# Attention tiles: four heads' scores in one chain with four banks, and values summed per query tile in one bank

## The chip, the cores and the metric

The kernel runs on one core of one Trainium2 chip. Its engines work side by side: TensorE multiplies matrices and transposes, VectorE and ScalarE do element work (ScalarE the exponentials), GpSimd helps, and the DMA queues move data. The engines take their own instructions in program order and wait for one another by semaphores. The metric is the time of the whole program in microseconds (us), measured on the device; the time before is the median of three runs.

## The reference, cut to what matters

Four batches of eight heads, 768 positions and 64 values per head go through attention, in which a query sees the 128 positions up to its own and, besides, the first four of its sequence. Its result is the input of a layer of eight experts of which each token uses one, and that of a last layer with a sigmoid gate.

```python
scores = scale * np.matmul(q, k.transpose(0, 1, 3, 2))
is_sink = pos[None, :] < int(n_sink)                 # n_sink = 4
rel = pos[:, None] - pos[None, :]
in_window = (rel >= 0) & (rel < int(window))         # window = 128
scores = np.where(is_sink | in_window, scores, -1000000000.0)
a = np.exp(scores - np.max(scores, axis=-1, keepdims=True))
a = a / (np.sum(a, axis=-1, keepdims=True) + 1e-09)
return np.matmul(a, v).astype(np.float32)
...
x = attention's result, 3072 tokens of 512
e_idx = np.argmax(x @ w_gate + bias, axis=1)         # top-1 of 8 experts, F = 1024
out[mask] = gate_w[mask, None] * (np.maximum(x[mask] @ w1[e], 0.0) @ w2[e])
h = out @ w_in; g = h * (1.0 / (1.0 + np.exp(-1.702 * h))); return g @ w_out
```

## The kernel before

**Tiles.** Attention takes the 3,072 queries in 24 tiles `t` of 128, six to a batch (NT = 6; i = t % NT is the tile's place in its batch). A tile's queries see their own 128 keys, the 128 keys of the tile before (none where i = 0) and the four sink keys, so a row of scores is 128 or, with i > 0, 260 wide. `c` counts the four pairs of heads, `g` the two halves of four heads, `a` the two heads of a pair.

**Steps of a tile.** `load` brings q, k and v two tiles ahead. `qtrans` and `ktrans` transpose q and k on TensorE, `qevac` (ScalarE) and `kevac` (VectorE) copy them from the accumulation banks to SBUF. `scores` multiplies two heads, one on rows 0 to 63 of the array and one on rows 64 to 127, each into a bank of its own. `mask` (VectorE, L202) adds the mask and finds the row's extreme, `expo` (ScalarE, L211) takes the exponential and its sum. `ptrans` transposes a pair's weights with four products (L224, L225; L227 where i = 0), `pevac` copies them into `pts`, on VectorE for odd pairs (L242) and on ScalarE for even ones (L244). `pv` multiplies them with the values, each head of a pair on 64 columns of the array, into `ops`. `sinksplit`, `sinktrans` (L258, tile `stp`) and `sinkevac` (L263) prepare the weights of the sinks. `oevac` (ScalarE, L291) copies `ops` to `oh`; `back` (tile `bt`, L298 for the sinks and L301) turns the result back to tokens and makes the expert logits, `norm` (VectorE, L319) divides by the sum and sends the tile to DRAM; `logits`, `then` and `pick` choose the token's expert.

**How values are summed before.** A half `g` has a bank of `ops` of its own, which holds two query tiles side by side. The values of key tile t-1 are multiplied once with the weights of query tiles t-1 and t together, a moving operand of 256 columns. So a query tile's sum is complete only when `pv` has run for two steps, and for a batch's last tile L284 adds products of 128 columns. Since the products accumulate into what stands there, ScalarE writes zeros into each half of a bank first (`zero`, L268). `pts` is one buffer of three places (NG = 3) that is never given back, and `where`, `pview` and `psrc` find a tile's place in it.

**Banks.** The accumulation memory has eight banks: three in a ring for scores (`s`, NS_BUFS), three in a ring with the tag "t" that all of `qp`, `kp`, `pt`, `stp` and `bt` share (NT_BUFS), and two for `ops`. A step that takes a bank of a ring waits until the copy that empties its former use is done.

**What sets the order.** Nothing is reordered by a compiler. Every step is an entry of the list `todo`, with a time in slots, four slots to a tile: the first slot `n` that it covers, plus an offset from the table `AT`. The list is sorted, and each engine gets its instructions in that order. `kinds` gives each kind its size, that is how many slots one call covers:

```python
for nm, (size, fn) in kinds.items():
    for n in range(0, 4 * T, size):
        t, c = divmod(n, 4)
        ...
        todo.append((n + AT[nm] - sooner, fn, (t,) if size == 4 else (t, c) if size == 1 else (t, c // 2)))
```

**The end of attention.** The first pair of experts starts while the last tiles finish: `OPEN` places its steps on the same line of slots (`x0` and `x1` transpose the first gathered tokens, L1130; `split*` split weights into two parts; `first0` and `first1` are the first products, L1166), and `MORE` places the steps that sort the first experts' tokens and later the search that spreads tokens over blocks. The product `o_pp` on TensorE gives the places of the first tokens (`perm`), with which GpSimd gathers them (`xg`). When the last tile's expert is chosen (`pk_oh`, L672), L824 counts all tokens and the routing proper begins. After this come the remaining pairs of experts and the last layer, nearly all of it on TensorE.

Of the kernel before, what the change touches and what calls it, by code (L numbers as in the profile page):

```python
# [6 lines left out]
F32 = mybir.dt.float32  # L7
# [21 lines left out]

AT = dict(sinkevac=13.229, oevac=13.14, qevac=-3.201, kevac=-0.864, scores=-0.497, mask0=0.153, mask1=0.329, expo0=0.53, ptrans=2.608, pevac=3.3,  # L30
          expo1=1.235, pv=6.555, qtrans=-4.329, ktrans=-1.83, back=14.129, sinktrans=12.315, norm=14.975, logits=18.7, then=19.826, pick=23.746,
          guard=7.159, invert=12.135, zero=5.2, sinksplit=8.053)
PVU = 2
LATE = 0


OPEN = dict(split1=2.989, x0=5.244, split0=4.299, x1=5.358, split2=5.494, split3=6.448, first0=6.769, first1=7.711, split4=14.718)
MORE = 85.058, 0.617, 92.724, 1.445


def attention(tc, cst, late, first, spare, q, k, v, wg, xd, then, pick, at_tile, more, opening):
# [8 lines left out]
    with ExitStack() as ctx:  # L50
# [32 lines left out]
        m0, m1, m2 = cst["m0"], cst["m1"], cst["m2"]  # L83
        NV, NG = 6, 3
        zs = per.tile([P, 1], F32, name="zs")
        nc.gpsimd.memset(zs, 0.0)


        pts = per.tile([P, NG, 4, 2, 2, P], F32, name="pts")
        ops = [ps_o.tile([P, 2, 2, P], F32, name=f"ops{i}") for i in range(2)]  # L90

# [89 lines left out]

        def scores(t, c):

            i = t % NT
            x = qt[t][0]
            for a in range(2):
                r = slice(64 * a, 64 * a + 64)
                ps = ps_s.tile([P, 512], F32, name=f"s{t}_{c}_{a}", tag="s")
                scs[(t, 2 * c + a)] = ps
                if i == 0:  # L190
                    ks, n = kts[r, c, 0, 0:P], P
                else:
                    ks, n = kts[r, c, i - 1 : i + 1].rearrange("p j k -> p (j k)")[:, 0 : KB + P], KB + P
                nc.tensor.matmul(ps[:, :n], x[r, c, :], ks, start=True, stop=True)  # L194
# [17 lines left out]

        def where(t, kk):

            return kk if t % NG else 1 - kk

        def ptrans(t, c):
            i = t % NT
            ps = ps_t.tile([P, 2, 2, P], F32, name=f"pt{t}_{c}", tag="t")
            k0, k1 = where(t, 0), where(t, 1)  # L220
            for a in range(2):
                h = 2 * c + a
                if i > 0:
                    nc.tensor.transpose(ps[:, k0, a, :], pn[t][:, h, 0:P], ident)  # L224
                    nc.tensor.transpose(ps[:, k1, a, :], pn[t][:, h, KB : KB + P], ident)  # L225
                else:
                    nc.tensor.transpose(ps[:, k1, a, :], pn[t][:, h, 0:P], ident)  # L227
            tps[("p", t, c)] = ps

        def pview(t, c, x):  # L230
            if t % NT == 0:
                return x[:, t % NG, c, :, t % 2, :]
            a, b = sorted(((t - 1) % NG, t % NG))
            return x[:, a : b + 1 : b - a, c, :, t % 2, :]

        def psrc(t, c):
            ps = tps[("p", t, c)]
            return ps[:, where(t, 1)] if t % NT == 0 else ps

        def pevac(t, c):  # L240
            if c % 2:
                nc.vector.tensor_copy(pview(t, c, pts), psrc(t, c))  # L242
            else:
                nc.scalar.activation(out=pview(t, c, pts), in_=psrc(t, c), func=AF.Copy)  # L244

# [24 lines left out]
        def pv(t, g=None):  # L270

            i = t % NT
            if i == 0:
                return
            kw = dict(start=False, stop=False, skip_group_check=True)
            for j in [t - 1] + ([t] if i == NT - 1 else []):
                for h in range(H) if g is None else range(4 * g, 4 * g + 4):

                    c, a = divmod(h, 2)
                    o = ops[c // 2][64 * a : 64 * a + 64, c % 2]  # L280
# [61 lines left out]
        def fill(n):  # L342
            for _ in range(n):
                nc.tensor.matmul(ops[1].rearrange("p c i t -> p (c i t)")[:, 0:256], cst["nothing"][:, 0:P], cst["nothing"], start=True, stop=True)

        fill(F1)

        def ok(t):
            return 0 <= t < T


        kinds = dict(sinkevac=(4, sinkevac), oevac=(2, oevac), qevac=(4, qevac), kevac=(4, kevac), scores=(1, scores), mask0=(1, lambda t, c: mask(t, 2 * c)),
                     mask1=(1, lambda t, c: mask(t, 2 * c + 1)), expo0=(1, lambda t, c: expo(t, 2 * c)), expo1=(1, lambda t, c: expo(t, 2 * c + 1)),
                     ptrans=(1, ptrans), pevac=(1, pevac), pv=(PVU, pv), qtrans=(4, qtrans), ktrans=(4, ktrans), back=(2, back), sinktrans=(4, sinktrans), norm=(2, norm), logits=(4, logits), then=(4, lambda t: then(t, lgs.pop(t))), pick=(4, pick), guard=(4, guard), invert=(4, invert), zero=(2, zero), sinksplit=(4, sinksplit))
# [3 lines left out]
        for g in range(2):  # L358
            todo.append((len(F2) + .001, zero, (0, g)))
        for nm, (size, fn) in kinds.items():  # L360
            for n in range(0, 4 * T, size):
                t, c = divmod(n, 4)
                if nm in ("qtrans", "qevac", "ktrans", "kevac", "zero") and t == 0 or nm.startswith("sink") and t % NT < 2:
# [46 lines left out]
        todo.append((last("scores", "mask0", "mask1"), close, (sctx, "scores")))  # L410
        todo.append((last("pv", "zero", "expo0", "expo1"), close, (tctx, "values")))
        for nm, time in OPEN.items():
# [27 lines left out]

NS_BUFS = 3
NT_BUFS = 3
# [1198 lines left out]
```

## Time and profile before

| what | value |
|---|---|
| median of 3 runs | 1136.49 us (1130.78 to 1139.29) |
| profiled execution | 1139.11 us, its span 1137.5 us |
| TensorE busy | 1082.0 us, 95% of the span |
| VectorE, ScalarE, GpSimd busy | 553.5, 418.1 and 242.8 us |
| granted TensorE clock | 0.975 of 2.4 GHz on average |
| attention | about the first 224 us of the span |

An engine's share over the whole span says little about one stage: VectorE's 49% is 72% within the attention and much less behind it. What a change is worth in a stage is read from that stage's rows: which engine has no idle time there, and for whom the others wait. In the rows below `PE` is TensorE, `DVE` VectorE, `ACT` ScalarE and `POOL` GpSimd. A form such as 64*128 64x260 means that 64 rows and 128 columns of the array are used and the moving operand has 260 columns; a product in full precision is done in several passes, so its count in the trace is twice that of the instructions.

### The profile page before, as it was taken

How to read it: one execution, taken by the hardware profiler on the slowest of the kernel's cores; microseconds unless marked ns; L12 is line 12 of the kernel's file. 1: busy time of each engine (PE TensorE's matmuls, PEld its weight loads, DVE VectorE, ACT ScalarE, POOL GpSimd, SP SyncE). 2: the span in 40 equal slices, each digit the busy share in tenths (PEclk: the TensorE clock that was granted, in tenths of full speed). 3: DMA queues.
4: the chain of work that ended last, by engine and by line, in shares of the span. 5: the costliest groups of instructions: out<-in, count | busy, mean ns of one | idle time of the engine just before them, and what ended most of it. 6: DMA issues, size and time to landing. Idle time of an engine off the chain costs nothing. (4 is left out here: it accounts for less than half of the span.)

```text
span 1137.5 us, 18802 instructions
## 1 busy us (share of the span) xinstructions
PE 1082.0 (95%) x6625; PEld 916.0 (81%) x6625; DVE 553.5 (49%) x1385; ACT 418.1 (37%) x1026; POOL 242.8 (21%) x397
## 2 busy tenths in 40 slices
PE   7999999888999999999869999999999999999996
PEld 4676766578998999999867888888888888888885
DVE  3776677785544484522102566656533334234242
ACT  4887887643222342222112323323323222223221
POOL 2523131452332233211100222222210011011011
PEclk8999999988988999999979999999999999999999
DMA  6667677642777865435666313112023023033010
GB/s 119 130 114 134 127 118 108 147 78 62 125 90 100 195 129 104 57 57 162 106 166 179 111 41 126 45 67 75 2 74 111 10 102 112 1 111 136 13 38 37
DMA packets 172115, 108.49 MB, mean 95 GB/s; under 512 B 118000, under 2 KB 149744, under 8 KB 171984
## 3 DMA queue, kind: packets, MB, share of 16 engines
q1 hardware_dynamic: 167184, 91.43, 38.3%
q0 software_dynamic: 4800, 15.49, 4.3%
q8 instruction: 60, 0.98, 0.4%
q14 instruction: 71, 0.58, 0.2%
HBM read 79.61 MB, written 27.29 MB: 94 GB/s over the span
## 5 line engine op out<-in xcount | busy, mean ns | idle before, releaser
L1166 PE MATMUL pu<-xh,wah 128*128 128x256 f32 (+1 forms) x576 | 187.3, 325 | 0.0
L1166 PE MATMUL pu<-xh,wal 128*128 128x256 f32 (+1 forms) x576 | 185.8, 323 | 0.4 <-DVEq L1275 0.4
L1166 PE MATMUL pu<-xl,wah 128*128 128x256 f32 (+1 forms) x576 | 185.7, 322 | 0.0
L1551 DVE TENSOR_TENSOR raw<-pu,raw 128x512 f32<-128x512 f32 x96 | 66.3, 691 | 244.8 <-ACT raw L1550 210.4
L1550 ACT ACTIVATE raw<-pu 128x512 f32<-128x512 f32 x96 | 57.4, 598 | 291.9 <-PE pu L1166 286.8
L1181 PE MATMUL pa<-h,wah 128*128 128x256 f32 x768 | 158.4, 288 | 5.1 <-issue 5.1
L1181 PEld LDWEIGHTS pa<-h,wah 128*128 128x128 f32 x768 | 130.3, 197 | 4.1 <-issue 4.1
L1166 PEld LDWEIGHTS pu<-xh,wal 128*128 128x128 f32 x576 | 112.2, 195 | 8.4 <-DVEq L1275 0.6
L1166 PEld LDWEIGHTS pu<-xh,wah 128*128 128x128 f32 x576 | 112.2, 195 | 8.3 <-issue 0.4
L1166 PEld LDWEIGHTS pu<-xl,wah 128*128 128x128 f32 x576 | 112.1, 195 | 7.5
L1181 PE MATMUL pa<-h,wal 128*128 128x256 f32 x384 | 110.6, 288 | 1.9 <-issue 1.9
L1189 ACT ACTIVATE h<-pu 128x256 fp32r<-128x256 f32 x96 | 36.9, 384 | 200.0 <-PE pu L1166 177.0
L1192 DVE SCALAR_TENSOR_TENSOR h<-pu,h 128x256 fp32r<-128x256 f32 x96 | 40.5, 422 | 125.2 <-ACT h L1189 64.5
L202 DVE CUSTOM_DVE_ANT_0 sc<-s,m 128x260 f32<-128x260 f32 (+1 forms) x192 | 73.1, 399 | 52.8 <-PE s L194 46.9
L211 ACT ACTIVATE pn<-sc,mx 128x260 f32<-128x260 f32 (+1 forms) x192 | 92.0, 483 | 5.2 <-DVE mx L202 4.7
L1118 ACT ACTIVATE h<-raw 128x512 fp32r<-128x512 f32 x96 | 60.7, 632 | 77.7 <-DVE raw L1551 77.7
L1181 PEld LDWEIGHTS pa<-h,wal 128*128 128x128 f32 x384 | 75.8, 197 | 3.4 <-issue 3.4
L1173 PE MATMUL pa<-wah,h 128*128 128x512 f32 x216 | 76.3, 389 | 0.0
L1173 PE MATMUL pa<-wbh,h 128*128 128x512 f32 x216 | 76.3, 389 | 0.0
L1166 PE MATMUL pu<-xh,wbh 128*128 128x512 f32 x192 | 74.8, 390 | 1.0 <-ACT y L1489 1.0
L1166 PE MATMUL pu<-xh,wbl 128*128 128x512 f32 x192 | 74.8, 390 | 0.0
L1166 PE MATMUL pu<-xl,wbh 128*128 128x512 f32 x192 | 74.8, 390 | 0.0
(327 smaller groups left out, 2067.8 us busy)
## 6 DMA issues: line engine op xcount, KB each, us to landing
raw<-in_moe_w_dram SPq DMA_DIRECT2D x64, 256.0 KB
cd<-yb SPq DMA_DIRECT2D x20, 512.0 KB
xd<-xe SPq DMA_DIRECT2D x24, 256.0 KB
raw<-yp SPq DMA_DIRECT2D x12, 512.0 KB
qn<-in_q_dram SPq DMA_DIRECT2D x22, 256.0 KB
kn<-in_k_dram SPq DMA_DIRECT2D x22, 256.0 KB
vn<-in_v_dram SPq DMA_DIRECT2D x22, 256.0 KB
yb<-y SPq DMA_DIRECT2D x10, 512.0 KB
```

The costliest lines, as they stand in the source:

```text
L202: nc.vector.tensor_tensor_reduce(out=sc[:, :n], in0=ps[:, :n], in1=m[:, :n], scale=1.0, scalar=3.0e38, op0=ALU.add, op1=ALU.min, accum_out=mx)
L211: nc.scalar.activation(out=pn[t][:, h, :n], in_=sc[:, :n], func=AF.Exp, scale=-1.0, bias=mx, accum_out=sums[t][:, h : h + 1])
L1118: A.activation(out=hi, in_=x, func=AF.Copy)
L1166: nc.tensor.matmul(ps[:, 0:n], w[a][:, s], cols(x, b, k), start=(k == 0 and i == 0), stop=(k == 3 and i == 2))
L1173: nc.tensor.matmul(acc, h[a][:, s], w[b][:, 512:], start=(f == 0 and j == 0), stop=(f == last and j == 2))
L1181: nc.tensor.matmul(acc[:, i % 2 * 256 : i % 2 * 256 + 256], wa[f][a][:, s], h[b], start=(f == 0 and i % 2 == 0 and j == 0), stop=(f == CH ...
L1189: A.activation(out=hi, in_=ps, func=AF.Relu)
L1192: V.scalar_tensor_tensor(out=lo, in0=ps, scalar=0.0, in1=hi.bitcast(F32), op0=ALU.max, op1=ALU.subtract)
L1550: A.activation(out=s, in_=ps, func=AF.Sigmoid, scale=1.702)
L1551: V.tensor_tensor(out=s, in0=ps, in1=s, op=ALU.mult)
```

## The change

`scores(t, g)` now makes the scores of four heads one behind the other, in four banks (NS_BUFS 3 to 4). `pv(t, g)` sums the values for its own query tile alone: for each head a product of 128 columns with the values of the tile before and one with those of its own, begun and ended in one bank `ops` that holds all eight heads of one query tile. The zeroing goes, `pts` becomes a tile of its own for each t (two buffers), and the eight banks are now four, three and one. The tables are new: `pv` moves from 6.555 to 7.004, and as a tile's sum is complete a tile earlier, `oevac` goes from 13.14 to 10.224, `back` from 14.129 to 10.991, `norm` from 14.975 to 11.395 and the steps behind them in the same way.

```diff
-AT = dict(sinkevac=13.229, oevac=13.14, qevac=-3.201, kevac=-0.864, scores=-0.497, mask0=0.153, mask1=0.329, expo0=0.53, ptrans=2.608, pevac=3.3,
+AT = dict(sinkevac=10.229, oevac=10.224, qevac=-2.123, kevac=-1.366, scores=-0.449, mask0=-0.2, mask1=0.21, expo0=0.692, ptrans=2.608, pevac=3.437,
...
-OPEN = dict(split1=2.989, x0=5.244, split0=4.299, x1=5.358, split2=5.494, split3=6.448, first0=6.769, first1=7.711, split4=14.718)
-MORE = 85.058, 0.617, 92.724, 1.445
+OPEN = dict(split1=4.183, x0=5.146, split0=3.966, x1=5.358, split2=5.428, split3=6.826, first0=6.763, first1=6.923, split4=14.582)
+MORE = 84.738, 0.617, 92.724, 1.62
...
-        ops = [ps_o.tile([P, 2, 2, P], F32, name=f"ops{i}") for i in range(2)]
+        ops = ps_o.tile([P, 4, P], F32, name="ops")
...
-        def scores(t, c):
+        def scores(t, g):
...
-            for a in range(2):
+            for c, a in ((2 * g, 0), (2 * g, 1), (2 * g + 1, 0), (2 * g + 1, 1)):
...
+            if c == 0:
+                pts[t] = p2.tile([P, 4, 2, 2, P], F32, name=f"pts{t}", tag="pts")
...
-        def zero(t, g):
-
-            nc.scalar.activation(out=ops[g][:, :, t % 2, :], in_=zs.unsqueeze(2).broadcast_to([P, 2, P]), func=AF.Copy)
...
-                    if j == t - 1:
-                        nc.tensor.matmul(o.rearrange("p i t -> p (i t)"), nat[j]["v"][:, h], pts[:, j % NG, c, a].rearrange("p i t -> p (i t)"), **kw)
-                    else:
-                        nc.tensor.matmul(o[:, t % 2, :], nat[j]["v"][:, h], pts[:, j % NG, c, a, t % 2, :], **kw)
+            for c in (2 * g, 2 * g + 1):
+                for kk in range(i == 0, 2):
+                    for a in range(2):
+                        nc.tensor.matmul(ops[64 * a : 64 * a + 64, c], nat[t - 1 + kk]["v"][:, 2 * c + a], pts[t][:, c, kk, a], start=(kk == 0 or i == 0), stop=(kk == 1), skip_group_check=True)
...
-            nc.scalar.activation(out=ohl[t][:, 2 * g : 2 * g + 2], in_=ops[g][:, :, t % 2, :], func=AF.Copy)
+            nc.scalar.activation(out=ohl[t][:, 2 * g : 2 * g + 2], in_=ops[:, 2 * g : 2 * g + 2], func=AF.Copy)
...
-NS_BUFS = 3
+NS_BUFS = 4
```

TensorE's order before, at the first half of tile 10 (`s10_1_0` is tile 10, pair 1, head 0 of it; `pt9_1` is tile 9, pair 1; `x4` counts like instructions, and the number behind a name is only its place in the program):

```order
L194 MATMUL s10_0_0_2439<-kts_1140,qt10_2327 128x260
L194 MATMUL s10_0_1_2441<-kts_1140,qt10_2327 128x260
L224 MATMUL pt9_1_2444<-ident_97,pn9_2353 128x128
L225 MATMUL pt9_1_2444<-ident_97,pn9_2353 128x128
L224 MATMUL pt9_1_2444<-ident_97,pn9_2353 128x128
L225 MATMUL pt9_1_2444<-ident_97,pn9_2353 128x128
L156 MATMUL qp11_2449<-ident_97,qn11_2330 128x128 x4
L301 MATMUL bt6_1_2467<-btw_1123,oh6_2368 128x144 x2
L194 MATMUL s10_1_0_2479<-kts_1140,qt10_2327 128x260
L194 MATMUL s10_1_1_2481<-kts_1140,qt10_2327 128x260
L282 MATMUL ops1_1130<-pts_1128,vn7_1787 64x256 x4
```

Each group of two heads stands by itself, with transposes and `bt6_1` between the two; the half's values come behind the second. The same place on TensorE with the change:

```order
L258 MATMUL ops_1126<-pts8_2367,vn7_1839 64x128 x2
L258 MATMUL ops_1126<-pts8_2367,vn8_1992 64x128 x2
L191 MATMUL s10_0_0_2502<-kts_1136,qt10_2387 128x260
L191 MATMUL s10_0_1_2504<-kts_1136,qt10_2387 128x260
L191 MATMUL s10_1_0_2506<-kts_1136,qt10_2387 128x260
L191 MATMUL s10_1_1_2508<-kts_1136,qt10_2387 128x260
L216 MATMUL pt9_1_2510<-ident_97,pn9_2415 128x128
L217 MATMUL pt9_1_2510<-ident_97,pn9_2415 128x128
...
L153 MATMUL qp11_2515<-ident_97,qn11_2398 128x128 x4
L216 MATMUL pt9_2_2542<-ident_97,pn9_2415 128x128
L217 MATMUL pt9_2_2542<-ident_97,pn9_2415 128x128
...
L275 MATMUL bt7_1_2560<-btw_1123,oh7_2469 128x144 x2
```

The two score groups, between which transposes stood, are now one, and it follows the half's value products; the step `back` of an earlier tile has moved from ahead of the second score group to behind the second pair's transposes, and it now takes the bank of the ring that `pt9_1` had three uses before.

TensorE's order before, at the end of attention, around the first expert products (`x0` makes `pu1` and `pu2`, `first0` and `first1` are the products of `pu0` and `pu1`, of which the first and the last ones stand here):

```order
L1130 MATMUL pu2_4357<-ident_97,xg1_82 128x128
L298 MATMUL bt22_0_4537<-svb3_3525,stt22_4517 128x288
L301 MATMUL bt22_0_4537<-btw_1123,oh22_4515 128x144 x2
L1166 MATMUL pu0_4355<-xh0_4344,wah0_4361 128x256
...
L1166 MATMUL pu1_4356<-xl0_4345,wah1_4363 128x256
L298 MATMUL bt22_1_4583<-svb3_3525,stt22_4517 128x288
L301 MATMUL bt22_1_4583<-btw_1123,oh22_4515 128x144 x2
L258 MATMUL stp23_4588<-identr_1124,st23_4474 96x128
L298 MATMUL bt23_0_4596<-svb3_3525,stt23_4594 128x288
L301 MATMUL bt23_0_4596<-btw_1123,oh23_4592 128x144 x2
L298 MATMUL bt23_1_4610<-svb3_3525,stt23_4594 128x288
L301 MATMUL bt23_1_4610<-btw_1123,oh23_4592 128x144 x2
```

A half's turn back to tokens (`bt22_0`) stands between `x0` and `first0`, and three more behind `first1`. The same place on TensorE with the change:

```order
L272 MATMUL bt22_0_4604<-svb3_3638,stt22_4601 128x288
L275 MATMUL bt22_0_4604<-btw_1123,oh22_4599 128x144 x2
...
L272 MATMUL bt22_1_4639<-svb3_3638,stt22_4601 128x288
L275 MATMUL bt22_1_4639<-btw_1123,oh22_4599 128x144 x2
...
L1102 MATMUL pu2_4504<-ident_97,xg1_82 128x128
L244 MATMUL stp23_4687<-identr_1124,st23_4631 96x128
L1138 MATMUL pu0_4502<-xh0_4491,wah0_4508 128x256
...
L1138 MATMUL pu1_4503<-xl0_4492,wah1_4510 128x256
L272 MATMUL bt23_0_4725<-svb3_3638,stt23_4691 128x288
L275 MATMUL bt23_0_4725<-btw_1123,oh23_4689 128x144 x2
L272 MATMUL bt23_1_4742<-svb3_3638,stt23_4691 128x288
L275 MATMUL bt23_1_4742<-btw_1123,oh23_4689 128x144 x2
```

Tile 22's turn back to tokens, half of which stood between `x0` and `first0` and half behind `first1`, has moved ahead of `x0`; behind `first1` only tile 23's is left. Ahead of `o_pp` now stand the sink transpose and the first half's `back` of tile 21 and one half of tile 22's values, which came behind it.

## Rows read from the trace of the kernel before

**Rows 1.** Windows, attention and after: busy us (instructions) by engine, clock, DMA

```profile
24.00:224.00 200.00, 198.94 (x1504) 135.43 (x1502) 144.08 (x598) 161.15 (x546) 66.01 (x208) 1.00 0.69 119
224.00:244.00 20.00, 11.47 (x80) 10.99 (x81) 12.75 (x27) 8.67 (x15) 10.21 (x13) 0.91 0.73 167
```

**Rows 2.** Waits of TensorE, 24 to 224 us: total, times, longest

```profile
PE stp L258 <- DVE pts L242: 0.6, 1, 0.6
```

**Rows 3.** Timeline of TensorE, one tile: start, us, operation, tiles, forms, count

```profile
94.48 0.27 PE L225 MATMUL pt<-ident,pn 128*128 128x128 f32 x1
94.68 0.71 PE L194 MATMUL s<-kts,qt 64*128 64x260 f32 x4
95.32 0.33 PE L224 MATMUL pt<-ident,pn 128*128 128x128 f32 x1
95.49 0.27 PE L225 MATMUL pt<-ident,pn 128*128 128x128 f32 x1
95.60 0.27 PE L224 MATMUL pt<-ident,pn 128*128 128x128 f32 x1
...
96.25 0.66 PE L301 MATMUL bt<-btw,oh 128*128 128x144 f32 x4
96.84 0.71 PE L194 MATMUL s<-kts,qt 64*128 64x260 f32 x4
97.48 1.08 PE L282 MATMUL ops<-pts,vn 128*64 128x256 f32 x8
98.49 0.33 PE L224 MATMUL pt<-ident,pn 128*128 128x128 f32 x1
```

**Rows 4.** Timeline of TensorE at a batch's last tile

```profile
67.33 1.08 PE L282 MATMUL ops<-pts,vn 128*64 128x256 f32 x8
68.25 0.61 PE L284 MATMUL ops<-pts,vn 128*64 128x128 f32 x8
68.79 0.44 PE L227 MATMUL pt<-ident,pn 128*128 128x128 f32 x2
```

**Rows 5.** Groups of instructions, 24 to 224 us: busy us, mean ns, idle before

```profile
L242 DVE COPY pts<-pt 128x512 f32<-128x512 f32 x40 | 27.6, 690 | 5.7 <-PE pt L225 4.7
...
L268 ACT ACTIVATE ops<-zs 128x256 f32<-128x256 f32 x46 | 17.8, 387 | 1.4
```

**Rows 6.** Timeline of VectorE: one score group, two stretches of the end

```profile
138.11 0.43 DVE L202 CUSTOM_DVE_ANT_0 sc<-s,m 128x260 f32<-128x260 f32 x1 [1.01 <-PE s L194]
...
138.60 0.69 DVE L242 COPY pts<-pt 128x512 f32<-128x512 f32 x1
...
216.10 0.64 DVE L242 COPY pts<-pt 128x512 f32<-128x512 f32 x1
...
237.82 2.38 DVE L675 CUSTOM_DVE_ANT_0 pk_d<-lg,bias 128x8 f32<-128x8 f32 x1 [0.30 <-POOL lg L330]
...
240.80 1.96 DVE L678 SCALAR_TENSOR_TENSOR pk_eq<-pk_d,pk_mx,c_rank 128x8 f32<-128x8 f32 x1
```

**Rows 7.** Timeline of TensorE: that score group, then the end

```profile
137.26 0.71 PE L194 MATMUL s<-kts,qt 64*128 64x260 f32 x4
...
216.80 0.27 PE L258 MATMUL stp<-identr,st 128*96 128x128 f32 x1 [0.58 <-DVE pts L242]
...
228.25 1.75 PE L1130 MATMUL pu<-ident,xg 128*128 128x128 f32 x7 [1.67 <-ACT xg L1139]
...
230.83 0.55 PE L1166 MATMUL pu<-xh,wah 128*128 128x256 f32 x1
...
233.98 0.29 PE L298 MATMUL bt<-svb,stt 96*128 96x288 f32 x1
...
236.03 0.37 PE L298 MATMUL bt<-svb,stt 96*128 96x288 f32 x1 [1.20 <-DVE xe L319]
...
237.26 0.38 PE L1166 MATMUL pu<-xh,wah 128*128 128x256 f32 x1
...
243.79 0.24 PE L824 MATMUL pt<-pk_oh,c_ones 128*128 128x192 bf16 x1 [3.41 <-DVE pk_oh L672]
```

More of the change, by code (lines that the diff above doesn't have):

```diff
@@ L83, in attention @@
         m0, m1, m2 = cst["m0"], cst["m1"], cst["m2"]
[L84 to L89, printed above, removed]
-        ops = [ps_o.tile([P, 2, 2, P], F32, name=f"ops{i}") for i in range(2)]
+        NV = 6
+        ops = ps_o.tile([P, 4, P], F32, name="ops")
+        pts = {}
         sctx = ctx.enter_context(ExitStack())
@@ L223, in ptrans @@
                 if i > 0:
-                    nc.tensor.transpose(ps[:, k0, a, :], pn[t][:, h, 0:P], ident)
-                    nc.tensor.transpose(ps[:, k1, a, :], pn[t][:, h, KB : KB + P], ident)
+                    nc.tensor.transpose(ps[:, 0, a, :], pn[t][:, h, 0:P], ident)
+                    nc.tensor.transpose(ps[:, 1, a, :], pn[t][:, h, KB : KB + P], ident)
                 else:
-                    nc.tensor.transpose(ps[:, k1, a, :], pn[t][:, h, 0:P], ident)
+                    nc.tensor.transpose(ps[:, 1, a, :], pn[t][:, h, 0:P], ident)
             tps[("p", t, c)] = ps
[L230 to L238, printed above, removed]
         def pevac(t, c):
+            if c == 0:
+                pts[t] = p2.tile([P, 4, 2, 2, P], F32, name=f"pts{t}", tag="pts")
+            k = slice(1, 2) if t % NT == 0 else slice(0, 2)
+            x, ps = pts[t][:, c, k], tps.pop(("p", t, c))[:, k]
             if c % 2:
-                nc.vector.tensor_copy(pview(t, c, pts), psrc(t, c))
+                nc.vector.tensor_copy(x, ps)
             else:
-                nc.scalar.activation(out=pview(t, c, pts), in_=psrc(t, c), func=AF.Copy)
+                nc.scalar.activation(out=x, in_=ps, func=AF.Copy)
         stt, sts = {}, {}
@@ L343, in fill @@
             for _ in range(n):
-                nc.tensor.matmul(ops[1].rearrange("p c i t -> p (c i t)")[:, 0:256], cst["nothing"][:, 0:P], cst["nothing"], start=True, stop=True)
+                nc.tensor.matmul(ops.rearrange("p c t -> p (c t)")[:, 0:256], cst["nothing"][:, 0:P], cst["nothing"], start=True, stop=True)
         fill(F1)
@@ L349, in ok @@
             return 0 <= t < T
-        kinds = dict(sinkevac=(4, sinkevac), oevac=(2, oevac), qevac=(4, qevac), kevac=(4, kevac), scores=(1, scores), mask0=(1, lambda t, c: mask(t, 2 * c)),
+        kinds = dict(sinkevac=(4, sinkevac), oevac=(2, oevac), qevac=(4, qevac), kevac=(4, kevac), scores=(2, scores), mask0=(1, lambda t, c: mask(t, 2 * c)),
                      mask1=(1, lambda t, c: mask(t, 2 * c + 1)), expo0=(1, lambda t, c: expo(t, 2 * c)), expo1=(1, lambda t, c: expo(t, 2 * c + 1)),
-                     ptrans=(1, ptrans), pevac=(1, pevac), pv=(PVU, pv), qtrans=(4, qtrans), ktrans=(4, ktrans), back=(2, back), sinktrans=(4, sinktrans), norm=(2, norm), logits=(4, logits), then=(4, lambda t: then(t, lgs.pop(t))), pick=(4, pick), guard=(4, guard), invert=(4, invert), zero=(2, zero), sinksplit=(4, sinksplit))
+                     ptrans=(1, ptrans), pevac=(1, pevac), pv=(2, pv), qtrans=(4, qtrans), ktrans=(4, ktrans), back=(2, back), sinktrans=(4, sinktrans), norm=(2, norm), logits=(4, logits), then=(4, lambda t: then(t, lgs.pop(t))), pick=(4, pick), guard=(4, guard), invert=(4, invert), sinksplit=(4, sinksplit))
         todo = []
@@ L357, in attention @@
             todo.append((n + AT["scores"] + .001, fill, (some,)))
-        for g in range(2):
-            todo.append((len(F2) + .001, zero, (0, g)))
         for nm, (size, fn) in kinds.items():
@@ L362, in attention @@
                 t, c = divmod(n, 4)
-                if nm in ("qtrans", "qevac", "ktrans", "kevac", "zero") and t == 0 or nm.startswith("sink") and t % NT < 2:
+                if nm in ("qtrans", "qevac", "ktrans", "kevac") and t == 0 or nm.startswith("sink") and t % NT < 2:
                     continue
@@ L410, in attention @@
         todo.append((last("scores", "mask0", "mask1"), close, (sctx, "scores")))
-        todo.append((last("pv", "zero", "expo0", "expo1"), close, (tctx, "values")))
+        todo.append((last("pv", "expo0", "expo1"), close, (tctx, "values")))
         for nm, time in OPEN.items():
```

17 lines of the change are left out of this document (3 added, 14 removed).

## Prediction

> **What bounds the kernel now.** I read first the windows of the attention [rows 1]: between 24 and 224 us TensorE is busy for 198.94 of 200 us, at the full clock (1.00, that is 2.4 GHz), while VectorE has 144.08 and ScalarE 161.15. Then the waits: in those 200 us TensorE waits for one thing once, 0.6 us [rows 2]. So in the attention the bound is TensorE's own stream. What is taken off its stream shortens the stage; what is taken off ScalarE or VectorE gives nothing as long as they keep up. Only behind it, from 224 to 244 us, does TensorE stand still: 11.47 of 20 us busy [rows 1]. There it waits for the gathered tokens, for VectorE and, 3.41 us long, for the last tile's choice [rows 7]. From then on it is again almost always at work, so that a shift of this point passes to the end. The sum is made against the profiled execution, 1139.11 us (span 1137.5), 2.6 above the median of 1136.49; I carry the difference over to the median.
>
> **Changes of shape on TensorE (a gain of 14.0 us).** Within tile 10 the same product costs more at its place than in a row [rows 3]. A transpose takes 0.11 us from start to start inside a group (95.49 to 95.60). By columns, 260 against 128, one pass of a score pair is 0.22, and the two passes of a group 0.44. But from the last transpose before the scores (94.48) to the second one behind them (95.49) it is 1.01 us, where 0.11 + 0.44 + 0.11 = 0.66 would do: a visit from transposes on 128 rows to scores on 64 rows and back costs 0.35. The longer visit, scores, then values on 64 columns, then transposes, costs 0.49 by the same reading: 96.25 to 98.49 is 2.24, of which `bt`, four times 0.12 at its 144 columns, takes 0.48, scores 0.44 and values 0.88 (four passes of two heads at 0.22), which leaves 0.44; with the slow first transpose (0.05 more) it is 0.49. A tile now makes two visits of each kind, 1.68 us in all. With the change scores and values still meet, in the other order, and the lonely score groups are gone: two visits of the long kind, 0.98. Saved: two times 0.35, 0.70 per tile, in the 20 tiles with 260-wide scores 14.0 us. The step from values straight to scores is in no row. Its cost lies between nothing (0.10 less per half: the entry of 0.20 at 94.48 to 94.68 less the usual 0.11) and a full visit of its own (0.20 more per half); I take the reverse order's, its nearest row. For the four tiles with 128-wide scores I count nothing: their groups have no row here, and 0.3 each is the most.
>
> **Values with 128 columns (nothing).** Each instruction of 256 columns becomes two of 128, each with its own weight load. At a batch's last tile both kinds stand next to each other [rows 4]: eight records of 256 columns take 0.92 to the next start, eight of 128 columns 0.54 including the way out. Both together take 1.46, and the wide ones alone took 1.01 [rows 3], so the narrow ones add 0.45, half of a wide group's 0.88 and a hair. The columns in all stay the same, and so does the time. The Trainium skill ("TensorE: Matmul & The Clock Gate", section "Back-to-back issue gap") speaks against the change: the spacing of load and multiply pairs is set by both, about 81 ns at 128 columns and 131 at 512, so that a narrow product is dearer per column. By an even line between these two figures, an estimate, 256 columns are 98 ns, and two narrow ones would cost 1.65 times a wide one. By that the value groups would grow from 0.88 to 1.45, 0.57 per half, 22.8 us in 20 tiles; that is the last rival below, against which the narrow group speaks [rows 4].
>
> **Zeroing (nothing).** 17.8 us of ScalarE go [rows 5], but TensorE does not wait for ScalarE. What this gives is room on ScalarE, 161 to about 143 us of a stage that itself gets shorter.
>
> **A new wait at the ring of three banks (a loss of 3.2 us).** In a half the order is now scores, four transposes, q (or k), four transposes, `back`. `back` needs the bank that the first four transposes filled, and thus VectorE's copy of it; before, a score group and the values lay between. From the chain's start: 0.64 for the first two heads with the way in and out [rows 3] and 0.44 for the others, so the transposes start at 1.08, the fourth at 1.08 + 0.17 + 0.22 = 1.47, and it ends 0.27 later [rows 3], at 1.74. VectorE has by then just made two masks: the first starts 0.85 behind a score group's start (137.26 to 138.11), lasts 0.43, and the next follows it [rows 6, 7], which ends near 1.65. Its copy lasts 0.69 [rows 5, 6] and TensorE goes on 0.06 after such a copy has ended (216.74 to 216.80) [rows 6, 7]: ready at 2.51. `back` could start at 1.08 + 0.49 + 0.44 + 0.44 = 2.45, since four transposes take 0.49 after scores and 0.44 in a row. The wait is 0.06 to 0.08 per half; I take 0.08, times 2 and 20. Behind `back` stand the values and the next score chain, for which masks and exponentials wait, so nothing hides it. Its ends are 0, if the copy is that much earlier, and 0.19, if the way into the scores costs 0.10 less, as above; but then the first term is larger by the same, and the two ends cancel.
>
> **The four score banks.** There is no spare bank: the next chain's last two heads use banks that this chain's last two masks must have left. On VectorE the copy ends at 2.46, the two masks behind it at about 3.3, and where a copy of keys, of the same size, comes before one of them, near 4.0; the next chain comes about 4.2 later and needs these banks half a microsecond after that. I count nothing, with that slack as the cover; its loss is a rival.
>
> **The end of attention (nothing, net).** Ahead of `o_pp` now stand a sink transpose (0.2), half a `back` (0.6 by 96.25 to 96.84, with its sink product 0.8) and half a tile of values (0.9): 1.9 us later, with everything that the gathered tokens start [rows 3, 7]. Against this, the `back` of tile 22 no longer stands between `x0`, which starts at 228.25, and `first0` at 230.83, about 0.8; and of the 3.28 us between the start of the first `back` behind `first1` (233.98) and the next expert product (237.26), of which 1.20 is a wait for VectorE, about 1.2 stay [rows 7]. TensorE's part is 2.9 us shorter. But L824 waits 3.41 us for VectorE's choice, whose steps are stretched to 2.38 and 1.96 us [rows 6], and how much this chain gives is in no row: from nothing to the whole 2.9, and with the stretching gone as much as 5. I take 1.9, which cancels the later `o_pp`, since the choice follows tile 23's `back`, which comes earlier.
>
> **The sum.** -14.0 + 3.2 + 1.9 - 1.9 = -10.8: 1128.3 for the profiled execution, 1125.7 on the median, 1.0% faster, at the edge of what a measurement of this kernel tells from no change (about 1%).
>
> **Rivals.** (1) More is gained: the ring's wait does not bind and the end gives its whole 5 us: -14.0 + 1.9 - 5 = -17.1, 1119. For it: the computed wait is a few hundredths. Against it: the 0.6 us in which TensorE did wait is for just this copy [rows 2]. (2) It is spent again: the step from values to scores costs a second full change, 0.20 per half (8.0 us), and `back` waits 0.19 (7.6): -14.0 + 8.0 + 7.6 + 1.9 - 1.9 = +1.6, 1138; with one of the two, 1130 to 1134. For it: each entry into a shape costs at its place, and nothing shows this one. (3) Slower: VectorE, which has 72% of the time [rows 1] of a stage that gets 5% shorter, falls behind within the half, and the chain waits for its last masks. It decides from a lag of 0.5 us, the slack above; one more copy of 0.69 or two masks ahead of it do it, and then each half stands about 0.5, 1.0 per tile, 24 us in 24 tiles: 1125.7 + 24 = 1150. Against it: the order on VectorE puts the masks nearly evenly. (4) Slower: each narrow product takes as long as the wide one, because its weight load bounds it; by 0.88 per half that is 35 us, 1161. Against it stands the narrow group [rows 4].
>
> **How the numbers follow.** The forecast has 0.45 (its own range 1119 to 1132, half of it on either side of 1125.1, where 1% begins), the larger gain 0.15, the spent gain 0.27, the VectorE lag 0.10, the dear narrow products 0.03. Faster by over 1% is the larger gain and half of the forecast, 0.38; slower 0.13; within 1% the rest, 0.49. The range goes from 1115, the first rival with the cheap step from values to scores (0.10 per half, 4 us), to 1139, the spent gain; it leaves the two slower cases out.
>
> **What would show it.** In the windows: attention ends about 9 us earlier with TensorE still over 97% busy. In TensorE's timeline of a tile: a score group of eight records of about 1.1 us, with no transposes between two groups, and value groups still near 1.0 (1.45 or more is rival 4). In TensorE's waits: a row of `bt` (or `stp`) for VectorE's `pts`, some 40 times, 3 us in all; 8 us would be rival 2. A row of TensorE `s` waiting for VectorE's `sc` or `mx` would be rival 3. At the end: `first0` closer behind `x0`, and L824's wait of 3.41. I am wrong if the chain's handshakes cost what the fewer changes of shape give, or if the step from values to scores is a full change.

## The result and the profile after

The changed kernel took 1115.11 us (median of 4 runs) beside 1135.45 for the kernel before on the same chip: a ratio of 0.983, 95% interval 0.980 to 0.986. That is 20 us, twice what was forecast (10.8), at the lower edge of the range (1115). The same kernel, measured twice more beside the kernel before, gave 1123.71 (0.991, 0.987 to 0.994) and 1122.82 (0.992, 0.989 to 0.995): 9 to 10 us. The three medians of the kernel before in these sets were 1135.45, 1134.02 and 1133.16, so the first set is the odd one on the changed kernel's side.

The windows that answer to [rows 1], from the changed kernel's profile:

```profile
24.00:224.00 200.00, 194.56 (x1835) 155.17 (x1833) 143.56 (x600) 150.46 (x500) 65.83 (x210) 0.99 0.84 128
224.00:244.00 20.00, 16.72 (x110) 16.05 (x110) 16.92 (x49) 9.05 (x17) 11.29 (x8) 0.82 0.43 84
```

TensorE has idle time by now, but the first window no longer lies within the attention: the last tile's scores start at 201.72 us where it was 206.59. TensorE's waits in it are still few; the first row, for the gathered tokens `xg`, belongs to the end of attention, and without it they come to 1.2 us (0.6 before [rows 2]):

```profile
PE pu L1102 <- ACT xg L1111: 3.7, 2, 3.4
PE pt L216 <- DVE pts L228: 0.6, 2, 0.3
PE o_pp L737 <- DVE raw L731: 0.4, 1, 0.4
PE bt L275 <- ACT oh L265: 0.2, 1, 0.2
```

Tile 10 on TensorE, which answers to [rows 3], and VectorE beside it, which answers to [rows 6]:

```profile
92.48 1.15 PE L191 MATMUL s<-kts,qt 64*128 64x260 f32 x8
93.56 0.33 PE L216 MATMUL pt<-ident,pn 128*128 128x128 f32 x1
...
94.71 0.27 PE L216 MATMUL pt<-ident,pn 128*128 128x128 f32 x1
94.82 0.27 PE L217 MATMUL pt<-ident,pn 128*128 128x128 f32 x1
95.09 0.73 PE L275 MATMUL bt<-btw,oh 128*128 128x144 f32 x4
95.75 1.09 PE L258 MATMUL ops<-pts,vn 128*64 128x128 f32 x16
96.78 1.15 PE L191 MATMUL s<-kts,qt 64*128 64x260 f32 x8
97.85 0.27 PE L244 MATMUL stp<-identr,st 128*96 128x128 f32 x1
```

```profile
93.33 0.43 DVE L199 CUSTOM_DVE_ANT_0 sc<-s,m 128x260 f32<-128x260 f32 x1 [0.95 <-PE s L191]
...
94.26 0.69 DVE L228 COPY pts<-pt 128x512 f32<-128x512 f32 x1
```

The four heads are one group of eight records, 1.08 us to the next start, and the sixteen narrow value records take 1.03, as the eight wide ones did (1.01). Between the last transpose (94.82) and `bt` (95.09) lie 0.27 us where two transposes lie 0.11 apart. VectorE's copy starts at 94.26, 1.78 behind the chain's start, where the prediction has it (its end at 2.46 less 0.69), but `bt` starts 0.83 behind the copy's start, not 0.75. No wait is listed for it: the transpose's modelled end is 95.09, so the row shows no idle time, and only the distance of the starts does. Over 38 such places between 42 and 200 us the distance is 0.21 us on average; in the variant E2 below, where nothing waits, it is 0.06 (0.11 where the next row is L275, 0.03 where `bt` begins with the sinks' product L272).

The end of attention, which answers to [rows 7]:

```profile
210.01 0.44 PE L737 MATMUL o_pp<-o_bt,raw 128*128 128x2 f16 x12
...
222.67 1.75 PE L1102 MATMUL pu<-ident,xg 128*128 128x128 f32 x7 [3.35 <-ACT xg L1111]
...
224.33 0.52 PE L1138 MATMUL pu<-xh,wah 128*128 128x256 f32 x1
...
228.91 0.30 PE L272 MATMUL bt<-svb,stt 96*128 96x288 f32 x1
...
230.33 0.37 PE L1138 MATMUL pu<-xh,wah 128*128 128x256 f32 x1
...
236.72 0.26 PE L796 MATMUL pt<-pk_oh,c_ones 128*128 128x192 bf16 x1 [3.28 <-DVE pk_oh L644]
```

Against [rows 7], `o_pp` comes 5.7 us earlier (215.67 before), `first0` starts 1.66 behind `x0`'s last row where it was 2.58, the first `back` behind `first1` 1.42 ahead of the next expert product where it was 3.28, and L796 (L824 before) 7.07 us earlier, with its wait for VectorE's choice hardly changed (3.28, 3.41 before).

So only 7 of the profile's 24 us were there when the routing starts. To see where the others came from I counted TensorE's product records from L824 (L796) on; there are 4,950 of them in each kernel, in the same order, so that the same number is the same work. Start of the routing and length of five stretches, in us, from each run's trace (the fillings are explained with the experiments):

```
run                          routing  0-500  500-930  930-2360  2360-2700  2700-4949
before                        243.8    66.4    68.4     171.0      65.2      512.7
changed                       236.7    66.3    55.4     171.0      61.0      512.8
E1  changed again             237.6    67.7    52.4     174.1      66.8      512.8
E11 changed, third time       237.6    67.1    53.4     172.6      66.0      512.8
E2  groups of two             242.7    66.4    57.4     171.0      64.7      512.8
E3  shared copy               242.1    66.4    53.4     172.4      66.9      512.8
E8  back behind the values    235.1    66.5    56.1     175.4      61.9      512.7
E5  before again              242.4    65.0    60.2     170.9      66.3      512.7
E6  before, new OPEN, MORE    243.8    68.0    59.4     172.8      66.2      512.8
E9  before, 128 fillings      244.0    65.9    60.5     171.1      65.7      512.7
E7  before, 59 fillings       244.9    67.2    55.5     172.9      66.2      512.7
E10 before, 59 fillings again 246.0    66.2    54.2     173.0      61.9      512.7
E4  changed, 69 fillings      235.7    66.1    58.1     171.9      73.2      513.0
E12 changed, 69, again        236.1    66.5    61.2     171.1      63.4      512.8
```

The stretch from 500 to 930 (the first pairs of experts behind the search) gave 13 us of the first profiles' 24, where I had counted on a shift that just passes through. What TensorE waits for there, first in the profile before and then in the changed one, 290 to 385 us:

```profile
PE pa L1181 <- issue: 6.6, 8, 2.1
PE pt L1130 <- ACT xs L1149: 2.5, 2, 1.6
```

```profile
PE pu L1138 <- issue: 1.6, 4, 0.4
```

The largest stop of the profile before looks like this in TensorE's timeline: products 1.4 us apart, with the weight load of each 0.70 ahead of it, and no releaser:

```profile
312.85 0.28 PE L1181 MATMUL pa<-h,wah 128*128 128x256 f32 x1 [2.15 <-issue]
314.25 0.37 PE L1181 MATMUL pa<-h,wal 128*128 128x256 f32 x1 [1.12 <-issue]
315.64 0.37 PE L1181 MATMUL pa<-h,wah 128*128 128x256 f32 x1 [1.03 <-issue]
```

### The profile page after: what moved, and what is told of

It reads as the page before. It is cut to its first block, busy times and chain, and to the rows that moved or that the text cites. A ratio compares the mean times of both kernels' runs of the same rounds, so it can differ in the third digit from the quotient of the medians.

```text
span 1113.2 us, 19356 instructions
## 1 busy us (share of the span) xinstructions
PE 1069.4 (96%) x6945; PEld 928.7 (83%) x6945; DVE 551.3 (50%) x1385; ACT 405.8 (36%) x978; POOL 243.1 (22%) x396
## 4 chain that ended last, share of the span: by engine, by line
PE 46%; issue 4%; DMA 1%; POOL 0%; POOLq 0%; ACT 0%; DVE 0%; SPq 0%; ACTq 0%
PE pu L1138 22%; PE pa L1145 16%; PE pu L1145 5%; DMA raw<-in_moe_w_dram 1%; PE pu L1450 1%; PE pa L1459 1%; POOL out_dram L1547 0%; POOLq L1609 0%; PE pt L1102 0%; DVE raw L1523 0%; ACT raw L1522 0%; ACT ca L1452 0%; POOLq L1547 0%; SPq L1067 0%; ACTq L1522 0%
## 5 line engine op out<-in xcount | busy, mean ns | idle before, releaser
L1522 ACT ACTIVATE raw<-pu 128x512 f32<-128x512 f32 x96 | 57.4, 598 | 291.8 <-PE pu L1138 290.3
```

The lines of the kernel that those rows point to most:

```text
L1522: A.activation(out=s, in_=ps, func=AF.Sigmoid, scale=1.702)
```

## Experiments

All are compared with the kernel before on the same chip; medians in us, ratio with its 95% interval. A batch is the time from the first scores of one batch's first tile to the next batch's, here from the third to the fourth: 51.51 before, 49.76 with the change, within 0.01 in every profile of either.

**E1, the changed kernel again** (no edit).

> The changed kernel unaltered, as the base of this set. The changed kernel's first profile ended 24 us earlier than the profile of before; only 7.1 us of it were there when the routing starts (the product with the last tile's choice, 243.79 to 236.72), and 12.6 us more came between 303 and 377 us of before, where TensorE stood with no releaser named. If that later gain belongs to the change, this run is again near 1115 us with only short stops of TensorE between 290 and 370 us; if it is chance from execution to execution, the stops come back here or the time moves by 5 us or more.

Measured: 1123.71, ratio 0.991. The stops stayed away, stretch 500 to 930 took 52.4 us, the routing started at 237.6, yet the time was 8.6 us above the first set. In the traces the difference lies in 930 to 2700 (8.9 us more). In that stretch TensorE stood 18.8 us where it stood 11.9 in the first profile (the longest wait is L1450's for expert weights, `in_moe_w_dram`: 10.5 us against 8.0), and it was busy for 222.1 us at a granted clock of 0.96 against 220.1 at 0.98. So the stretch from 500 to 930 is the change's in some way, and another part of the first 20 us was not.

**E2, scores in groups of two.**

```diff
-        def scores(t, g):
+        def scores(t, pair):
...
-            for c, a in ((2 * g, 0), (2 * g, 1), (2 * g + 1, 0), (2 * g + 1, 1)):
+            for c, a in ((pair, 0), (pair, 1)):
...
-        kinds = dict(... scores=(2, scores), ...
+        kinds = dict(... scores=(1, scores), ...
```

> The changed kernel with the scores again in groups of two heads, the second group at the slot where a second pair's step stands; values, banks and tables as changed. It puts one lonely visit to the scores' shape back into each half tile. Theory A (changes of shape are the gain): 0.35 us per half more on TensorE, about 0.7 per tile, less the wait of the turn back to tokens for the copy (0.16 per half in the changed kernel's profile), which the visit covers: a batch of six tiles goes from 49.8 to about 52 us, the attention ends 7 to 9 us later, the time is near 1123. Theory B (the gain is from elsewhere, such as the freed zeroing or the narrow values): the batch stays within 0.5 us of 49.8.

Measured: 1127.91, ratio 0.995 (0.992 to 0.997); batch 51.61, routing at 242.7. The timeline of its tile:

```profile
95.32 0.33 PE L216 MATMUL pt<-ident,pn 128*128 128x128 f32 x1
...
96.34 0.71 PE L191 MATMUL s<-kts,qt 64*128 64x260 f32 x4
96.98 0.33 PE L216 MATMUL pt<-ident,pn 128*128 128x128 f32 x1
...
97.37 0.27 PE L217 MATMUL pt<-ident,pn 128*128 128x128 f32 x1
97.47 0.66 PE L275 MATMUL bt<-btw,oh 128*128 128x144 f32 x4
98.06 1.09 PE L258 MATMUL ops<-pts,vn 128*64 128x128 f32 x16
99.08 0.71 PE L191 MATMUL s<-kts,qt 64*128 64x260 f32 x4
99.72 0.27 PE L244 MATMUL stp<-identr,st 128*96 128x128 f32 x1
```

The lonely group is back (96.34, between transposes), and `bt` follows the last transpose at 0.10, without a wait. The batch is 1.85 us longer than with the chain and the same as before (51.51): the chain is all of the attention's gain, and the new sums, the narrow products and the missing zeroing together are worth nothing, as forecast. Theory A. The attention ended 5.7 us later than in the first changed profile (last tile's scores at 207.44), less than the 7 to 9 expected, and the time was 4.2 us above E1. It was still 6.1 us below the kernel before, though the attention took as long: a second source, to which E7 comes.

**E3, the odd copy shared by two engines.**

```diff
             if c % 2:
-                nc.vector.tensor_copy(x, ps)
+                nc.vector.tensor_copy(x[:, :, 0], ps[:, :, 0])
+                other_half[(t, c)] = x[:, :, 1], ps[:, :, 1]
```

A new step `pevac2`, 0.31 slots behind `pevac`, copies `other_half` on ScalarE.

> The changed kernel with each odd pair's copy of the transposed weights shared: VectorE copies one head, ScalarE the other. It is there to take away the wait of the turn back to tokens for VectorE's copy, which costs about 0.16 us per half tile in the changed kernel's profile (0.27 us between two starts where 0.11 would do). Theory A (that wait is on the path): 0.16 times two times 20, about 6 us less, the batch goes from 49.8 to 48.2 us. Theory B (ScalarE, now 78% busy in the attention, takes the part of VectorE): the wait changes its name from VectorE to ScalarE, and the batch stays at 49.8 us or grows.

Measured: 1127.58, ratio 0.994 (0.993 to 0.996); batch 51.33, 1.57 more than with the change. `bt` now stands 0.33 behind the last transpose, and ScalarE's half (L227) waits for VectorE's (L235):

```profile
96.69 0.39 ACT L227 ACTIVATE pts<-pt 128x256 f32<-128x256 f32 x1 [0.24 <-DVE pts L235]
...
96.79 0.27 PE L217 MATMUL pt<-ident,pn 128*128 128x128 f32 x1
97.12 0.76 PE L283 MATMUL bt<-btw,oh 128*128 128x144 f32 x4
```

Theory B, but not for want of time on ScalarE: the two halves never ran side by side. In none of the 48 pairs does ScalarE's half start before VectorE's has ended, in 42 it starts 0.03 to 0.05 us behind that end, although ScalarE stood idle ahead of most of them. What makes it wait is not shown; the experiment says nothing of a copy that is really shared. The distance to `bt` got 0.13 longer on average (0.34 against 0.21), and ten halves of that are 1.3 of the batch's 1.57 us, which fits a wait that is on TensorE's path; but this edit lengthens it.

**E8, `back` behind the values.**

```diff
-          ... back=10.991, ...
+          ... back=11.02, ...
```

> The changed kernel with the turn back to tokens a hair later in the slots, so that it stands behind the half's values and not ahead of them; nothing else changes. The bank that it takes has then long been copied. It costs one more change between whole-array and value shapes, since values no longer meet the scores: by the changed kernel's rows 0.64 instead of 0.57 us per half. Theory A (the wait for the copy, 0.16 per half, is on the path): 0.16 less 0.07, 0.09 per half, the batch goes from 49.76 to about 48.9 us. Theory B (whoever is late only moves: the norm behind it delays the masks): the batch stays at 49.8 or grows.

Measured: 1118.24, ratio 0.987 (0.983 to 0.990); batch 49.73. Its timeline:

```profile
92.86 1.15 PE L191 MATMUL s<-kts,qt 64*128 64x260 f32 x8
...
95.19 0.27 PE L217 MATMUL pt<-ident,pn 128*128 128x128 f32 x1
95.40 1.09 PE L258 MATMUL ops<-pts,vn 128*64 128x128 f32 x16
96.42 0.76 PE L275 MATMUL bt<-btw,oh 128*128 128x144 f32 x4
97.11 1.15 PE L191 MATMUL s<-kts,qt 64*128 64x260 f32 x8
```

The wait is gone: 0.21 to the values, which is what the step into their shape costs, and `bt` follows them at once. But `bt`, which by the prediction's count has 0.48 us of products, now takes 0.69 between two changes of shape. This half is 4.25 us (92.86 to 97.11) against 4.30 (92.48 to 96.78): the wait was worth 0.16 and the extra change of shape costs 0.11, not 0.07. Three more halves of the batch gain 0.04 to 0.05, the others together lose nearly as much, and the batch hardly moves. That is theory B's result, but the rows give another reason: the change of shape takes most of what the wait gives. Against the changed kernel itself it was not timed on one chip.

**E5, the kernel before again, E6, the kernel before with the changed OPEN and MORE, E7, the kernel before with 59 more filling products.**

The edit of E7 puts 79 products of 64 columns in the place of 20 of 256, ahead of the first tile; E6's new tables are those of the change. TensorE's instructions come in by transfers of 256 each (last section), and E7 moves the borders between them.

```diff
-        fill(F1)
+        for _ in range(F1 + 59):
+            nc.tensor.matmul(ops[1].rearrange("p c i t -> p (c i t)")[:, 0:64], cst["nothing"][:, 0:P], cst["nothing"][:, 0:64], start=True, stop=True)
```

> The kernel before, unaltered, for a second profile of it. Between the products number 500 and 930 behind the routing's start (310 to 379 us) its first profile lost 12 us more than all five profiles of the changed kernel and its variants, in stops of TensorE with no releaser named. Theory S (the stops belong to the kernel before): this profile has them again, the stretch from product 500 to 930 again takes about 68.4 us against 55.4. Theory C (chance from one loading or execution to the next): the stretch takes about 55 to 57 us and the stops are gone or stand elsewhere; then the changed kernel's real gain is the part ahead of the routing, 6 to 8 us.

> The kernel before with the two tables OPEN and MORE of the changed kernel, that is with the opening of the experts and the search placed as there, and the attention as before. If these tables take away the stops between 310 and 379 us, the stretch from product 500 to 930 takes 55 us here and 68 in the kernel before, and the time falls by about 10 us; if they do no more than place the start, the routing starts within 2 us of 243.8 us and the time stays within 0.5%.

> The kernel before with 59 more, shorter filling products of the same columns in all ahead of the first tile: 118 more instructions of TensorE, which move the borders of its 256-instruction transfers to where they lie in the changed kernel. Theory I (the stops hang on these borders): the stops between 310 and 379 us vanish, 10 us less. Theories S by another cause, or C: the stretch behaves as in the unaltered kernel before.

Measured: E5 1133.89, ratio 1.000 (0.998 to 1.003), stretch 60.2; E6 1135.19, ratio 1.002 (1.000 to 1.004), stretch 59.4; E7 1129.41, ratio 0.994 (0.991 to 0.998), stretch 55.5. The first profile's 68.4 was an outlier by 8 us (theory C holds for that part), and the tables of the opening give nothing. The windows of the stretch, columns as in [rows 1], for the first profile, E5 and E7:

```profile
310.20:378.60 68.40, 59.25 (x433) 58.02 (x432) 25.89 (x54) 15.32 (x32) 19.43 (x20) 0.88 0.75 102
```

```profile
307.40:367.60 60.20, 52.59 (x433) 51.63 (x432) 25.79 (x54) 15.31 (x32) 18.07 (x18) 1.00 0.86 110
```

```profile
312.10:367.60 55.50, 53.84 (x433) 53.01 (x432) 25.86 (x54) 15.28 (x32) 18.04 (x18) 0.97 0.82 113
```

Of the 8.2 us between the first two, 6.7 are the clock: the same products keep TensorE busy for 59.25 us at a granted clock of 0.88 (in part at 1.2 GHz) and for 52.59 at 1.00; without work it stands 9.2 and 7.6 us. In E7 it stands 1.7 us, as in the changed kernel's first profile (1.6). So 59 more fillings ahead of the first tile made the kernel before 5 us faster, and its stretch the same as the changed kernel's.

**E4, the changed kernel with 69 more fillings** (the same edit with 89 products of 57 columns).

> The changed kernel with 69 more, shorter filling products of the same columns in all ahead of the first tile, where TensorE has nothing else to do: 138 more instructions on TensorE, nothing else changed. TensorE's instructions come in by transfers of 16 KB, one for each 256 instructions in the trace, and the number of added instructions brings these borders behind the attention back to where they lie in the kernel before. Theory I (the stops of before between 310 and 375 us hang on where these borders fall): the stops come back, 5 us of stops and as much again by the lower clock behind them, time near 1124 to 1128. Theory II (they hang on the time at which the steps run beside the transfers of weights): nothing changes, 1115.

Measured: 1127.66, ratio 0.993 (0.989 to 0.996), 4.0 above E1; stretch 58.1. Toward theory I, but the interval overlaps E1's.

**E9 to E12, the control and the repeats**: the kernel before with 128 fillings more (E9, 148 products of 34 columns) and with 59 again (E10), the changed kernel (E11) and with 69 again (E12).

> The kernel before with 128 more, shorter filling products of the same columns in all ahead of the first tile: 256 more instructions of TensorE, exactly one transfer's worth, so that the borders behind the attention lie where they lie unaltered. It is the control of the run with 59. Theory I (where the borders fall sets what the experts' first pairs lose): as the unaltered kernel before, within 3 us of it, and the stretch from product 500 to 930 at 59 to 68 us. Theory F (more filling as such, a warmer start or other timing, gave the 5 us): faster by about 5 us, as the run with 59.

> The kernel before with 59 more filling products again, the borders as in the changed kernel. Theory I: about 5 us faster than the kernel before and than the run with 128, the stretch from product 500 to 930 near 55.5 us as in the first run of it and in the changed kernel. Chance: no difference from the run with 128.

> The changed kernel unaltered, a third time: base for the run beside it. The first time it was 20 us faster than the kernel before, the second time 10. Stretch from product 500 to 930 at 52 to 56 us; time between 1115 and 1124.

> The changed kernel with 69 more filling products again, the borders as in the kernel before. Theory I: about 4 to 5 us slower than the changed kernel beside it, as in the first run (1127.7 against 1123.7). Chance: no difference of more than 2 us.

Measured: E9 1133.82, ratio 1.002 (0.999 to 1.004), stretch 60.5; E10 1128.33, ratio 0.996 (0.994 to 0.998), stretch 54.2; E11 1122.82, stretch 53.4; E12 1124.71, ratio 0.993 (0.990 to 0.996), stretch 61.2. More filling as such does nothing (E9), a shift of the borders does (E10): theory I for the kernel before, 5.5 us between the two. On the changed kernel the stretch behaves the same way, but the time moved by 1.9 us only, which this set doesn't tell from none. Waits of TensorE from 290 to 385 us in E9, E10 and E12, in this order:

```profile
PE pt L1131 <- ACT xs L1150: 5.7, 2, 3.1
PE pa L1182 <- issue: 2.2, 2, 2.0
```

```profile
PE pu L1167 <- issue: 2.0, 2, 1.8
```

```profile
PE pt L1103 <- ACT xs L1122: 5.2, 2, 3.1
PE pu L1139 <- issue: 2.1, 2, 1.8
```

With the borders of the kernel before (before, E5, E6, E9, E4, E12) TensorE waits 2.5 to 5.7 us for the gathered tokens' tile `xs`, and the stretch takes 58.1 to 68.4 us; with the others (changed, E1, E2, E3, E7, E8, E10, E11) it waits 0 to 2.0 us for it, and the stretch takes 52.4 to 57.4. The two sets don't overlap.

The tokens themselves are not late. ScalarE weighs them (`xs<-xs`) right behind its step `h`, 0.1 to 0.2 us after its end in all runs, and it is `h` that comes late, in E5 (first) and not in the changed kernel:

```profile
360.67 0.28 PE L1166 MATMUL pu<-xl,wah 128*128 128x256 f32 x1
...
363.77 0.38 ACT L1189 ACTIVATE h<-pu 128x256 fp32r<-128x256 f32 x1 [5.28 <-PE pa L1181]
364.36 0.72 ACT L1149 ACTIVATE xs<-xs 128x512 f32<-128x512 f32 x1 [0.20 <-ACTq L1380]
```

```profile
354.30 0.28 PE L1138 MATMUL pu<-xl,wah 128*128 128x256 f32 x1
354.66 0.38 ACT L1161 ACTIVATE h<-pu 128x256 fp32r<-128x256 f32 x1 [2.54 <-PE pu L1138]
```

`h` reads TensorE's `pu`. It starts 0.36 us behind the start of the last product of `pu` in the changed kernel, and 3.10 behind it in E5. At the two places of the stretch where `xs` is due (products 706 and 910) the distance is 2.5 to 3.8 us in all six runs with the borders of before, and 0.3 to 0.4 in the other eight, but for one place each in E2 (2.4) and E8 (2.0). So TensorE waits there for its own product, which ScalarE could use only that much later.

## Why the prediction was right, and where it was not

**Changes of shape: right.** The lonely visits were priced at 0.70 per tile, 3.5 per batch of five such tiles. E2 against the changed kernel gives 1.85 per batch net of the ring's wait; ten waits of 0.16 (0.211 less the 0.055 without one) make it 3.4. The step from values straight to scores, which no row of before has, costs no more than the reverse one: read as in the forecast, the long visit is 0.50 in E2 (97.47 to 99.72), against 0.49. In the changed kernel it is 0.57 (95.09 to 97.85); the 0.07 more stand at `bt` behind its wait, which takes 0.66 to the next start, and 0.59 in E2.

**The ring's wait: right in its place, too small by half.** Counted at 0.08 per half, it is 0.16 on average, 6.2 us in all and not 3.2. The copy started when computed; what was off is the time from its start to TensorE's next product, 0.83 us here, which I had put at 0.75 from a copy of 0.69 and a release of 0.06. This is most of the difference at `o_pp`: 8.9 us forecast, 5.7 measured.

**Values, zeroing, score banks: right.** The narrow products cost nothing (E2: 51.61 against 51.51; sixteen records in 1.03 us against eight wide ones in 1.01, [rows 3]), and no product row of TensorE's `s` waits for VectorE, so the third and fourth rival have nothing. The two figures that the Trainium skill ("TensorE: Matmul & The Clock Gate", section "Back-to-back issue gap") gives for 128 and 512 columns do not carry over to these products.

**The end of attention: right.** From `o_pp` to L824 the forecast was 1.9 us less; it is 1.4 (28.12 to 26.71), with the two named gaps shorter by 0.9 and 1.9 us.

**The step that failed** is the first part's last sentence on the bound, that behind the routing's start TensorE is almost always at work and a shift passes to the end. At the routing's start 10.8 us were forecast and 7.1 measured; behind it the experts' first pairs gave about 5 more. So the sum, 10.8, came near the two later sets (9 to 10 us) with two errors that cancel: the larger wait took 3, and the first pairs gave what was not in the sum. That is luck, and it is luck too that the first set's median lies inside the range, by 0.1 us.

The new value products bring 320 more product records, with their weight loads 640 on TensorE, and this moves the borders between its instruction transfers (see the last section). That such a move by itself is worth about 5 us in the kernel before is shown by E7 and E10 against E9. E2 and E3 point the same way: they have the changed kernel's borders and a batch as long as before (51.61 and 51.33), and are 6 us faster than the kernel before. That the change owes its 5 us to it is seen in the stretch of the table, where both kernels take the long form with the one set of borders and the short form with the other, and in the time only weakly (4.0 us in E4, 1.9 in E12).

**What stays open.** Why the first set gave 20 us and not 10. The kernel before was the same in all sets; the changed kernel's first profile is shorter than E1's from 930 to 2700 by 8.9 us, 6.9 of them time in which TensorE stands, and that stretch, in which it waits for expert weights, spreads from 232 to 245 us over all runs with no tie to the borders or the change. Nor is it shown how a transfer's place delays TensorE's products.

## What to carry to other kernels

Where TensorE is the bound, price an instruction by its neighbours: here the same score group cost 0.35 us more between transposes than next to another group, and an order that lets like shapes meet pays even when it adds a wait elsewhere. Read waits from the distance between starts too, since a pipelined row's modelled end can hide one. And before a few microseconds far behind an edit are put down to it, compare the granted clock and the idle time of that stretch over a second profile, and move the instruction count alone, with a control that adds one whole transfer.

## What the runs showed of the hardware that was not expected

TensorE's instructions come in by transfers of about 16 KB, which the page of the profile counts under the queue q8 (0.98 MB in 60 packets for the kernel before). That they are TensorE's follows from their number: 61 with 256 instructions more on this engine (E9), 62 with the change's 640.

```profile
q8 instruction: 60, 0.98, 0.4%
```

```profile
q8 instruction: 61, 1.00, 0.4%
```

In the kernel before, 118 more instructions in an idle place made the program 5 us faster, and 256 changed nothing measurable (E10 and E9, ratios 0.996 and 1.002). In the traces of E5, E9, E12 and the first one of before, one such transfer in the stretch from 290 to 385 us, close behind the issue of a gather of tokens, took 6.7, 4.5, 5.5 and 5.8 us, where the median is 1.0 to 1.1. But E11, whose stretch is short, has one of 4.4 us too, and E6 and E4, whose stretches are long, have none above 1.4: a long transfer is not what tells the two forms apart. The places where TensorE stops in the stretch from 500 to 930 are the same in all runs, near products 498 to 509, 701 to 706 and 908 to 910. With the borders of before it stops at all three; with the others it stops at the last two only once each, in E8 and E2.
